# The exponentials' loads of the kernel generation: GpSimd's queue in place of SyncE's

## The chip, the cores and the metric

The kernel runs on one core of a Trainium2 chip. The core has five engines, each with its own instruction stream: TensorE (PE in the profile; its weight loads are PEld), VectorE (DVE), ScalarE (ACT), GpSimd (POOL) and SyncE (SP). SyncE, ScalarE and GpSimd also issue DMAs, which sixteen DMA engines carry out. The metric is the time of one execution on the device, in microseconds (us). TensorE's clock can be lowered by a throttle; the profile gives the granted clock as a share of full speed.

## The reference

The forward part, cut to what is computed; the kernel also returns the gradients for its twelve inputs, pulled back from `grad_out`.

```python
x = A_u                                            # 1 x 2048 x 576, bf16
xn = layernorm(x)
# state space branch
dt = exp(log_dt)[:, None]
P = exp((dt * A)[:, :, None] * arange(2048))       # A complex, 576 x 128
K = einsum("dn,dnl,dn->dl", C, P, dt * B).real     # one convolution kernel per channel
s = irfft(rfft(pad(xn)) * rfft(pad(K)))[:2048] + xn * Dskip
# gated branch
h = silu(xn @ w1) * (xn @ w3)                      # w1, w3: 576 x 4608
out = x + s * silu(h @ w2)                         # w2: 4608 x 576
...
out, vjp = jax.vjp(f, ...)
return out, *vjp(grad_out)
```

## The kernel before

The kernel is written with a framework that takes the program in the order in which Python produces it, gives each instruction a due time (`self.at(us)`), and lays out one fixed stream per engine from the due times and the data dependences. `issue_after` fixes an order between two instructions by hand, and `Chain` does so for a row of DMAs on one queue: each stands behind the one before it in the stream. Pools of buffers (`bufs=`) give the number of tiles of a name that may be in flight; a tile's load waits until the last reader of the tile that had its buffer is done.

The program has four parts: a preparation (layernorm, the spectrum of the input, and the exponentials of `early_exps`, which are stored to `E_dram`), then the stage with which this document deals, then the convolution with the second product of the gated branch, and the backward part.

In that stage two streams of work are interleaved.

*The kernel generation*, `ssm_kernel`, goes over 36 chunks of 16 channels with due times 6 us apart (TK). A chunk loads its exponentials E_l (L755; 128x1280 bf16, 320 KB, pool `kg_e` with three buffers) from `E_dram`. Then `kgen_chunk` makes five selector matmuls of the phases into PSUM (L776, et_ps, three buffers), ScalarE takes their sines into cs_k (L778, five instructions, two buffers), and VectorE multiplies and adds: p_k (L785), q_k (L789), two t_k (L797) and v_k (L801). In the streams, p_k and q_k are the first and the last reader of E_l. SyncE stores p_k for every second chunk (L787, `PZ_dram`) and q_k for each (L793, `Q_dram`, 512 KB). `kgen_sum` contracts q_k and v_k on TensorE (the kps products, L818) two chunks later, and copies the result to KT (L830). `phase_rows` (L726) fetches the phases' rows, lhs_t, in twelve small DMAs on SyncE, in front of the chunks 2, 11 and 20. At chunk 20 the matrix of the transform is made on VectorE and GpSimd (`dft_kernel_matrix`).

*The gate steps*, `ffn_hidden`, are 72, of two token tiles each, eight for every block of 512 hidden columns. A step multiplies with w1 and w3 (pg and pu, the matmuls of 128 rows in L1122, those of the last 64 rows, called tail matmuls here, in L1131). ScalarE makes s_t (silu, L1137) and u_t (L1142), VectorE g_t (L1141) and h_t (L1145). SyncE stores h_t (L1148), GpSimd stores g_t and u_t (L1151, 256 KB each). g_t, u_t, s_t and h_t have three buffers each. A block's weights are loaded once, on SyncE, into one of two buffers; those of the second block are chained behind `self.kg_load`, which at that point is the load of chunk 2. The gate steps start five ahead of the chunks, and `gate_mark` puts the first matmul of a step behind the last selector matmul of a chunk.

Some loads and stores for later stages also hang on `el`, the name that a chunk's E load has. `conv_loads`: at chunk 8 a row of Dskip and a store of a matrix, chained on SyncE; at chunk 12 the DMA copy `odd_grad_out`, within DRAM, on ScalarE's queue, behind the sine that was issued last (`self.sin_last`); at chunk 18 four transposes on SyncE. `turned_loads`: at chunk 25 a store, at chunk 30 eight transposes, all chained on SyncE.

SyncE's queue in this stage holds E loads, lhs_t loads, gate weights, PZ, Q and H stores and the chained ones, in one stream; each waits at the head of it for what it needs. GpSimd's holds the G and U stores.

Of the kernel before, what the change touches and what calls it, by code (L numbers as in the profile page):

```python
# [101 lines left out]
class K:  # L102
# [627 lines left out]
    def ssm_kernel(self, T0, TK, ps, ps1):  # L730
        nc, cfg = self.nc, self.cfg
        D, N = cfg.D, cfg.N
        NCH, H = D // 16, D // 2
        TW = 16 * (cfg.AV // 2 + cfg.BV)
        assert self.GE[-1] == NCH and cfg.AV == 2 * cfg.LT
        with self.pool(name="kg_l", bufs=2) as lp, \
                self.pool(name="kg_e", bufs=3) as ep, \
                self.pool(name="kg_qv", bufs=4) as qvp, \
                self.pool(name="kg_sb", bufs=2) as sb, self.pool(name="kg_dft", bufs=1) as dp:
            prev, lhs = [], [self.lhs_0]  # L740
            self.marks = []
            self.at(T0 - 3)
            self.write_weights(nc.scalar, self.WT[1], [self.W1[:, k] for k in range(2)])
            self.double_weights(nc.vector, self.WT[1])
            for ch in range(NCH):
                yield T0 + TK * ch
                self.at(T0 + TK * ch)
                if ch == 20:
                    self.dft_kernel_matrix(dp)
                if ch + 6 in self.GE[1:-1]:  # L750
                    lhs.append(self.phase_rows(len(lhs), lp, "lhs_t"))
                if ch in self.GE:
                    g = self.GE.index(ch)
                E = ep.tile([P, TW], BF16, name="E_l")
                el = self.kg_load = nc.sync.dma_start(out=E[:], in_=self.E_dram[ch // 4, :, ch % 4 * TW:(ch % 4 + 1) * TW])  # L755
                if ch in (8, 12, 18):
                    self.conv_loads(el, (8, 12, 18).index(ch))
                if ch in (25, 30):
                    self.turned_loads(el, (25, 30).index(ch))
                qv = self.kgen_chunk(ch, E, lhs[g][:, ch - self.GE[g], :], sb, qvp, ps)  # L760
                prev.append(qv)
                if ch >= 2:
                    self.kgen_sum(ch - 2, prev.pop(0), ps1, T0 + TK * ch, TK)
            for i in range(2):
                yield T0 + TK * (NCH + 0.5 * i)
                self.kgen_sum(NCH - 2 + i, prev.pop(0), ps1, T0 + TK * (NCH + 0.5 * i), TK * 0.5)

    def kgen_chunk(self, ch, E, lhs, sb, qvp, ps):
        nc, cfg = self.nc, self.cfg
        AV, BV = cfg.AV, cfg.BV  # L770
        DC, AP = 16, AV // 2
        QW, TW = DC * BV, DC * (BV + AP)
        CS = sb.tile([P, 2, TW], BF16, name="cs_k")
        for o in [QW, *range(0, QW, 256)]:
            pt = ps.tile([P, 2, 256], FP32, name="et_ps")
            ins = nc.tensor.matmul(pt[:], lhsT=lhs, rhs=self.SEL[:, :, o:o + 256], start=True, stop=True)  # L776
            with self.tc.issue_after(self.exps_last.ins):
                self.sin_last = nc.scalar.activation(out=CS[:, :, o:o + 256], in_=pt[:].bitcast(I16)[:, :, 0::2], func=ACT.Sin,  # L778
                                                     scale=6.283184 / 2 ** 16)
        self.marks.append(ins)  # L780
        q = qvp.tile([P, DC, 2, BV], BF16, name="q_k")
        if ch % 2 == 0:
            self.p2 = sb.tile([P, 2, 2, DC * AP], BF16, name="p_k")
        p = self.p2[:, ch % 2]
        nc.vector.tensor_tensor(out=p, in0=CS[:, :, QW:], in1=E[:, QW:][:, None].to_broadcast([P, 2, DC * AP]), op=ALU.mult)  # L785
        if ch % 2:
            nc.sync.dma_start(out=self.PZ_dram[:, ch - 1:ch + 1].rearrange("p j r x -> p (j r x)"),  # L787
                              in_=self.p2[:].rearrange("p j r x -> p (j r x)"))
        nc.vector.tensor_tensor(out=q[:].rearrange("p d k b -> p k d b"),  # L789
                                in0=CS[:, :, 0:QW].rearrange("p k (d b) -> p k d b", b=BV),  # L790
                                in1=E[:, 0:QW].rearrange("p (d b) -> p d b", b=BV)[:, None]
                                .to_broadcast([P, 2, DC, BV]), op=ALU.mult)
        nc.sync.dma_start(out=self.Q_dram[ch], in_=q[:].rearrange("p d k b -> p (d k b)"))  # L793
        t = sb.tile([P, 2, 2, DC, AV], BF16, name="t_k")
        for s in range(2):
            w = self.WT[s][:, ch].rearrange("p k r e u -> p (k r e) u")
            nc.vector.tensor_tensor(out=t[:].rearrange("p k r e (s a u) -> p (k r e) s a u", s=2, u=2)[:, :, s],  # L797
                                    in0=p.rearrange("p r (e a) -> p (r e) a", a=AP)[:, None].to_broadcast([P, 2, 32, AP]),
                                    in1=w[:, :, None, :].to_broadcast([P, 64, AP // 2, 2]), op=ALU.mult)
        v = qvp.tile([P, 2, DC, AV], BF16, name="v_k")  # L800
        self.v_last = nc.vector.tensor_tensor(out=v[:].rearrange("p k e a -> p k (e a)"),  # L801
                                              in0=t[:, :, 0].rearrange("p k e a -> p k (e a)"),
                                              in1=t[:, :, 1].rearrange("p k e a -> p k (e a)"), op=ALU.add)
        return q, v
# [1429 lines left out]
```

## Time and profile before

| what | value |
|---|---|
| time of the runs | 1758.15, 1758.81 and 1772.55 us, median 1758.81 |
| the profiled execution | 1755.24 us, of which the profile's span is 1753.1 |
| busy, share of the span | PE 1625.1 us (93%), DVE 1402.1 (80%), ACT 916.1 (52%), POOL 422.0 (24%) |
| hardware queue of SyncE's and ScalarE's DMAs | 565324 packets, 264.49 MB |
| software queue of GpSimd's DMAs | 37088 packets, 109.31 MB |

The stage in which both streams run goes from the first p_k, at 137.10 us, to the last, at 372.79. In front of it the gate steps run alone with the end of the preparation, behind it come the rest of the gate steps, the convolution and the backward part:

| stretch (us) | PE busy | DVE busy |
|---|---|---|
| 0 to 110 | 90.65 | 73.56 |
| 110 to 137 | 24.30 | 12.86 |
| 372.8 to 480 | 100.92 | 96.82 |
| 480 to 1753 | 1200.33 | 1014.99 |

How to read the rows that follow. A row of the timeline has start, duration, engine, line, operation, output and inputs, shapes, and the number of equal instructions that follow each other and are put in one row; in brackets stands the idle time in front of it and what ended it. SPq, ACTq and POOLq are the engines' DMA issues, where the duration is the issue and not the transfer. A row of the waits names the waiting instruction, what released it, the total, the number and the largest of these waits in the window. A row of the windows gives, for a stretch of time, the busy time of each engine with the number of its instructions, TensorE's mean granted clock, the DMA engines' busy share and the data rate.

### The profile page before, as it was taken

To read this page: it belongs to the slowest core of one execution; us is meant where nothing else is said; L and a number is where in the kernel's file an instruction comes from. 1 tells how busy PE (TensorE), PEld (TensorE's weight loads), DVE (VectorE), ACT (ScalarE), POOL (GpSimd) and SP (SyncE) were. 2 spreads that over 40 slices of the span, in tenths; PEclk is the share of its full clock that TensorE was granted. 3 is DMA by queue.
4 is the path that set the end of the run, shared out by engine and by line. 5 is a ranking of instruction groups with operands and counts; after the bars stand their busy time and mean duration, and the time that the engine had idled before them with its cause. 6 is when DMAs were issued, how large, how long until landed. Compare 5 with 4: busy or idle time off the path is not lost. (4 is left out here: it accounts for less than half of the span.)

```text
span 1753.1 us, 33144 instructions
## 1 busy us (share of the span) xinstructions
PE 1625.1 (93%) x12786; PEld 981.8 (56%) x12841; DVE 1402.1 (80%) x2170; ACT 916.1 (52%) x1674; POOL 422.0 (24%) x639
## 2 busy tenths in 40 slices
PE   7798788999997899889999999999999998999998
PEld 4453333444443677646555655555455566777766
DVE  6657798989894565587995899679799966899897
ACT  5667678777773111565866767565655501111111
POOL 7142121222223211111111212112121352122143
PEclk8899999999998999999999999999999999999999
DMA  6568897998778989848495776769899999999992
GB/s 204 208 210 288 287 314 257 322 340 259 254 264 208 232 208 191 225 144 235 146 278 161 206 205 202 196 172 268 196 262 225 251 222 240 227 205 216 231 201 51
DMA packets 624363, 394.86 MB, mean 225 GB/s; under 512 B 426798, under 2 KB 565678, under 8 KB 624206
## 3 DMA queue, kind: packets, MB, share of 16 engines
q1 hardware_dynamic: 565324, 264.49, 61.5%
q0 software_dynamic: 37088, 109.31, 19.8%
q10 hardware_dynamic: 21794, 18.95, 3.5%
q8 instruction: 100, 1.64, 0.4%
q14 instruction: 57, 0.47, 0.1%
HBM read 122.18 MB, written 182.13 MB: 174 GB/s over the span
## 5 line engine op out<-in xcount | busy, mean ns | idle before, releaser
L2017 PEld LDWEIGHTS <-acts 128*128 128x128 bf16 x2304 | 223.6, 98 | 63.9 <-issue 3.3
L1965 PE MATMUL pgw<-ggu,xn_bf 128*128 128x512 bf16 x1152 | 254.0, 379 | 0.1
L1122 PEld LDWEIGHTS <-xnT 128*128 128x128 bf16 x1152 | 107.8, 98 | 156.1 <-issue 53.5
L1500 DVE TENSOR_TENSOR pr_q<-et_ps,pz 128x1024 f32<-128x1024 f32 x144 | 176.0, 1223 | 21.1 <-PE et_ps L1494 11.9
L1965 PEld LDWEIGHTS <-xn_bf 128*128 128x128 bf16 x1152 | 111.5, 98 | 131.0 <-issue 0.4
L1504 DVE TENSOR_REDUCE S_b<-pr_q 128x64 f32<-128x1024 f32 x144 | 175.4, 1218 | 3.9
L1877 PE MATMUL ph<-w2T,goT 128*128 128x512 bf16 (+3 forms) x800 | 159.5, 368 | 10.6 <-DVE e L1237 3.7
L1122 PE MATMUL pg<-wmB_w,xnT 128*128 128x512 bf16 x539 | 151.5, 383 | 15.7 <-DVE g_t L1141 11.2
L1122 PE MATMUL pu<-wmB_w,xnT 128*128 128x512 bf16 x558 | 151.3, 383 | 1.7 <-issue 0.8
L1943 PE MATMUL pgw<-go_o,h_n 128*128 128x288 bf16 x1152 | 149.7, 287 | 1.1 <-ACT gh L1895 0.8
L1943 PEld LDWEIGHTS <-h_n 128*128 128x128 bf16 x1152 | 111.1, 98 | 31.2 <-issue 1.0
L1137 ACT ACTIVATE s_t<-pg 128x512 bf16<-128x512 f32 x144 | 87.2, 606 | 75.4 <-PE pu L1131 60.1
L2017 PE MATMUL px<-wT_ggu,acts 128*128 128x288 bf16 x896 | 123.5, 291 | 2.5 <-DMA wT_ggu<-in_B_w_dram 2.5
L1877 PEld LDWEIGHTS <-goT 128*128 128x128 bf16 (+1 forms) x800 | 65.0, 99 | 96.2 <-issue 41.1
L1151 POOL DMA_DIRECT2D G_dram<-g_t x72 | 52.3, 727 | 258.8 <-DVE g_t L1141 135.3
L1485 ACT COPY gz<-gz 64x1024 bf16<-64x1024 bf16 x36 | 37.6, 1043 | 147.1 <-DMA gz<-gK_dram 88.2
L2017 PE MATMUL px<-wA,acts 128*128 128x288 bf16 x832 | 109.8, 286 | 0.5 <-ACT gw13t L1980 0.5
L1971 POOL DMA_DIRECT2D out_dram<-gw x72 | 51.9, 722 | 207.6 <-ACT gw L1967 181.0
L778 ACT ACTIVATE cs_k<-et_ps 128x512 bf16<-128x512 int16 x180 | 93.2, 618 | 14.2 <-PE et_ps L776 11.5
L1948 POOL DMA_DIRECT2D out_dram<-gw x36 | 20.0, 555 | 330.6 <-ACT gw L1947 324.0
L1142 ACT CAST u_t<-pu 128x512 bf16<-128x512 f32 x144 | 86.4, 600 | 11.7 <-PE pu L1122 9.6
L1837 DVE TENSOR_TENSOR ggu<-ggu,h_n 128x1024 bf16<-128x1024 bf16 x72 | 48.9, 686 | 44.6 <-ACT ggu L1849 44.5
(341 smaller groups left out, 3190.4 us busy)
## 6 DMA issues: line engine op xcount, KB each, us to landing
G_dram<-g_t POOLq DMA_DIRECT2D x72, 256.0 KB, 4.5
U_dram<-u_t POOLq DMA_DIRECT2D x72, 256.0 KB, 4.7
H_dram<-h_t SPq DMA_DIRECT2D x72, 256.0 KB
Q_dram<-q_k SPq DMA_DIRECT2D x36, 512.0 KB
ggu<-G_dram POOLq DMA_DIRECT2D x18, 1024.0 KB, 8.1
h_n<-U_dram POOLq DMA_DIRECT2D x18, 1024.0 KB, 8.8
GG_dram<-ggu SPq DMA_DIRECT2D x36, 512.0 KB
GU_dram<-ggu SPq DMA_DIRECT2D x36, 512.0 KB
```

The lines of the kernel that those rows point to most:

```text
L778: self.sin_last = nc.scalar.activation(out=CS[:, :, o:o + 256], in_=pt[:].bitcast(I16)[:, :, 0::2], func=ACT.Sin, scale=6.283184 / 2 ** 16)
L1122: ins = nc.tensor.matmul(pt[:], lhsT=xnT[:, c, ts], rhs=wm[w][:, c, :], start=(q == 0 and c == 0), stop=(q == 1 and c == nfull - 1))
L1137: nc.scalar.activation(out=s_t[:, :, q, :], in_=pgv, func=ACT.Silu)
L1142: nc.scalar.copy(out=u_t[:, :, q, :], in_=puv)
L1151: self.u_stores[step] = nc.gpsimd.dma_start(out=dst[fb * ng:(fb + 1) * ng, i0 // 4, :, i0 % 4:i0 % 4 + NT, :].rearrange("g p t f -> p g (t ...
L1500: nc.vector.tensor_tensor(out=pr[:], in0=T[z][:].rearrange("p s k d f j -> p (s k) (d f j)")[:, None] .to_broadcast([P, 2, 4, 4 * AV]), in ...
L1504: nc.vector.tensor_reduce(out=self.sums_of[-1][:, :, :, z, :, dg, d0:d0 + 8].rearrange("p r s k d -> p (r s) k d"), in_=pr[:].rearrange("p ...
L1877: prev = nc.tensor.matmul(dst(j, k), lhsT=lw, rhs=rh, start=start, stop=stop)
L1943: self.pe_last = nc.tensor.matmul(pgw[pi_][:, 0:pw], lhsT=hn[:, tt, fl * P:(fl + 1) * P], rhs=self.go_o[:, tt, po:po + pw], start=(tt == 0 ...
L1965: self.pe_last = nc.tensor.matmul(pw_[:], lhsT=self.xn_bf[:, tt, c * P:(c + 1) * P], rhs=ggu[:, :, tt, :], start=(n == 0), stop=(n == LT - 1))
L1971: self.gp(lambda: nc.gpsimd.dma_start(out=aps[names[w]][(c - 1) * P:(c + 1) * P, fb:fb + FG].rearrange("(c p) f -> p c f", p=P), in_=gw[:, ...
L2017: self.pe_last = nc.tensor.matmul(px[pi_][:, 0:pw], lhsT=acts[i][:, ai, fi, :], rhs=w[:, po:po + pw], start=(n == 0), stop=(n == len(steps ...
```

## The change

Three edits. The E load goes from `nc.sync` to `nc.gpsimd`. The call of `kgen_chunk`, which stood after the hooks for later loads, stands before them. And `kg_load` and `el`, which named the E load of the chunk, now name its Q store, which is on SyncE: the second block's gate weights and the chained loads of `conv_loads` and `turned_loads` stand behind that instead. Since `kgen_chunk` has been called by then, `self.sin_last` in `conv_loads` is the last sine of chunk 12 instead of chunk 11. What is computed, the sizes and the buffers stay.

```diff
@@ -752,13 +752,14 @@
                 if ch in self.GE:
                     g = self.GE.index(ch)
                 E = ep.tile([P, TW], BF16, name="E_l")
-                el = self.kg_load = nc.sync.dma_start(out=E[:], in_=self.E_dram[ch // 4, :, ch % 4 * TW:(ch % 4 + 1) * TW])
+                nc.gpsimd.dma_start(out=E[:], in_=self.E_dram[ch // 4, :, ch % 4 * TW:(ch % 4 + 1) * TW])
+                qv = self.kgen_chunk(ch, E, lhs[g][:, ch - self.GE[g], :], sb, qvp, ps)
+                prev.append(qv)
+                el = self.kg_load = self.q_store
                 if ch in (8, 12, 18):
                     self.conv_loads(el, (8, 12, 18).index(ch))
                 if ch in (25, 30):
                     self.turned_loads(el, (25, 30).index(ch))
-                qv = self.kgen_chunk(ch, E, lhs[g][:, ch - self.GE[g], :], sb, qvp, ps)
-                prev.append(qv)
                 if ch >= 2:
                     self.kgen_sum(ch - 2, prev.pop(0), ps1, T0 + TK * ch, TK)
             for i in range(2):
@@ -790,7 +791,7 @@
                                 in0=CS[:, :, 0:QW].rearrange("p k (d b) -> p k d b", b=BV),
                                 in1=E[:, 0:QW].rearrange("p (d b) -> p d b", b=BV)[:, None]
                                 .to_broadcast([P, 2, DC, BV]), op=ALU.mult)
-        nc.sync.dma_start(out=self.Q_dram[ch], in_=q[:].rearrange("p d k b -> p (d k b)"))
+        self.q_store = nc.sync.dma_start(out=self.Q_dram[ch], in_=q[:].rearrange("p d k b -> p (d k b)"))
         t = sb.tile([P, 2, 2, DC, AV], BF16, name="t_k")
         for s in range(2):
             w = self.WT[s][:, ch].rearrange("p k r e u -> p (k r e) u")
```

## The prediction, made before the changed kernel ran

> **What bounds the kernel now.** I read the busy shares in three stretches first: the whole stage in which the change lies, and two stretches inside it where chunks follow each other evenly.
>
> ```profile
> core 0: us, PE busy (x) PEld busy (x) DVE busy (x) ACT busy (x) POOL busy (x), PEclk, DMA share, GB/s
> 137.10:372.80 235.70, 208.90 (x1923) 92.85 (x1955) 203.80 (x324) 180.44 (x357) 51.25 (x71) 0.97 0.89 301
> 230.80:268.00 37.20, 35.33 (x340) 16.20 (x345) 35.66 (x57) 30.75 (x62) 10.43 (x15) 1.00 0.96 318
> 329.70:372.80 43.10, 40.38 (x420) 18.89 (x428) 41.59 (x65) 33.85 (x68) 9.49 (x14) 1.00 0.99 312
> ```
>
> In the even stretches VectorE is busy 35.66 of 37.20 us (96%) and TensorE 35.33 (95%): the two together set the pace. Over the whole stage VectorE has only 203.80 of 235.70 us (86%). So time is lost somewhere between, and the starts of p_k, the first VectorE instruction of a chunk, show where (numbered 0 to 35 in order of time; here 8, 10, 13, 19, 20, 21, 22, 28 and 35):
>
> ```profile
> 188.43 0.41 DVE L785 TENSOR_TENSOR p_k<-cs_k,E_l 128x512 bf16<-128x512 bf16 x1
> 200.68 0.42 DVE L785 TENSOR_TENSOR p_k<-cs_k,E_l 128x512 bf16<-128x512 bf16 x1
> 230.89 0.42 DVE L785 TENSOR_TENSOR p_k<-cs_k,E_l 128x512 bf16<-128x512 bf16 x1
> 267.96 0.42 DVE L785 TENSOR_TENSOR p_k<-cs_k,E_l 128x512 bf16<-128x512 bf16 x1
> 289.84 0.41 DVE L785 TENSOR_TENSOR p_k<-cs_k,E_l 128x512 bf16<-128x512 bf16 x1
> 292.51 0.42 DVE L785 TENSOR_TENSOR p_k<-cs_k,E_l 128x512 bf16<-128x512 bf16 x1
> 295.79 0.42 DVE L785 TENSOR_TENSOR p_k<-cs_k,E_l 128x512 bf16<-128x512 bf16 x1
> 329.70 0.43 DVE L785 TENSOR_TENSOR p_k<-cs_k,E_l 128x512 bf16<-128x512 bf16 x1
> 372.79 0.42 DVE L785 TENSOR_TENSOR p_k<-cs_k,E_l 128x512 bf16<-128x512 bf16 x1
> ```
>
> The even pace is (267.96 - 230.89 + 372.79 - 329.70) / 13 = 6.17 us per chunk. From 10 to 13 it took 30.2 us instead of 18.5, and from 19 to 20 21.9 instead of 6.2. The waits and SyncE's queue around the first hole:
>
> ```profile
> 190.06 1.23 DVE L789 TENSOR_TENSOR q_k<-cs_k,E_l 128x2048 bf16<-128x2048 bf16 x1
> 208.15 2.63 SPq L726 DMA_DIRECT2D lhs_t<-PCS_dram  x5
> 208.29 0.79 ACTq L627 DMA_DIRECT2D odd_grad_out<-in_grad_out_dram  x1
> 210.82 10.98 SPq L755 DMA_DIRECT2D E_l<-E_dram  x3
> DVE p_k L785 <- DMA E_l<-E_dram: 10.3, 1, 10.3
> SPq L755 <- DMA odd_grad_out<-in_grad_out_dram: 8.8, 1, 8.8
> PE pg L1122 <- DVE g_t L1141: 11.2, 6, 9.2
> ```
>
> The buffer for chunk 11 was free when q_k of chunk 8 ended, at 190.06 + 1.23 = 191.29. But in SyncE's order that load stands behind the last of twelve small lhs_t loads, which are themselves strung between H and Q stores that wait for VectorE. It went out at 210.82. VectorE stood in front of p_k for 10.3 us, and TensorE, which needed g_t from behind that p_k, for 9.2. The second hole has the same queue in it: chunk 20's load is behind the next twelve.
>
> ```profile
> 277.50 0.34 SPq L755 DMA_DIRECT2D E_l<-E_dram  x1
> ```
>
> **The change part by part.** The instruction orders of the two programs say what moves. All 36 loads are on GpSimd's queue, one between the G and U stores of each gate step; GpSimd gets no other work, SyncE loses 36 issues, and the sizes stay. After the stage, the order on each engine is the old one. So the sum is made over the stage, and what it loses or gains passes to the end.
>
> *The holes.* Load c+3 now goes out when q_k of chunk c ends, past SyncE's lhs_t, H, Q and weight entries. What it has left until its p_k, from an even stretch (p_k and q_k of chunk 14, p_k of chunk 17):
>
> ```profile
> 236.75 0.42 DVE L785 TENSOR_TENSOR p_k<-cs_k,E_l 128x512 bf16<-128x512 bf16 x1
> 239.14 1.22 DVE L789 TENSOR_TENSOR q_k<-cs_k,E_l 128x2048 bf16<-128x2048 bf16 x1
> 255.43 0.42 DVE L785 TENSOR_TENSOR p_k<-cs_k,E_l 128x512 bf16<-128x512 bf16 x1
> L1151 POOL DMA_DIRECT2D U_dram<-u_t x41: 725/725/727, 111.3 to 384.2; - x41
> DMA to landing us min/median/max: 2.6/5.1/7.6
> L1200 POOL DMA_DIRECT2D w2g<-in_B_w_dram x6: 704/722/722, 547.9 to 552.2; - x6
> DMA to landing us min/median/max: 6.9/10.8/11.8
> ```
>
> 255.43 - 240.36 = 15.07 us, less 0.73 for the issue: 14.3 us. A GpSimd load of E does not exist in the trace. Stores of 256 KB on that queue in this very stage land in 2.6 to 7.6 us; loads of 288 KB, six issued in a row, in 6.9 to 11.8. I take 7.6, the same stage at the same load; both ends are below 14.3, so the load is hidden by three chunks of VectorE work. If that cover is gone, the excess is paid on VectorE.
>
> Here the Trainium skill speaks against the change: SBUF — State Buffer, section "SBUF: two separate sides", says that a DMA from GpSimd's queue is starved of descriptors while VectorE runs a two-port performance-mode instruction, and a later section gives about 620 against 3100 ns. The row above does not show it: 41 issues between 725 and 727 ns with VectorE 86% busy. By the rule, 2.5 us more would make 7.6 into 10.1, still an estimate under the slack, and the sum would be the same.
>
> Without late loads, chunks 8 to 35 take 27 x 6.17 = 166.6 us, plus VectorE's once-only work for the kernel matrix at chunk 20:
>
> ```profile
> 270.00:280.00 10.00, 2.61 (x3) 1.02 (x1) 1.00 0.72 235
> ```
>
> That is 2.6, and some 0.5 for five tiny ones beside it: 169.7 us against 372.79 - 188.43 = 184.4. **Gain 14.7 us.** The bounds are +-3.6, an even pace that is 0.13 off.
>
> *The uneven places left.* In the new order the kps products still split the selector matmuls near chunks 13 and 19. That costs between 0 (the piece 8 to 10 runs at 6.13 with such a split) and 2 us. I take 1.
>
> *A new late piece near the start.* kg_load now names a Q store. So the gate weights of the second block go out behind the Q store of chunk 2, where they went out behind its E load; and the order reacts: 18 selector matmuls (chunks 3 to 5 and part of 6) now stand ahead of step 8's first gate matmul, where eight stood. Step 8 before, and the price of a gate step without a chunk:
>
> ```profile
> 150.79 1.43 SPq L87 DMA_DIRECT2D wmB_w<-in_B_w_dram  x2
> 153.18 5.23 ACT L778 ACTIVATE cs_k<-et_ps 128x512 bf16<-128x512 int16 x10
> 156.02 1.02 PE L1122 MATMUL pg<-wmB_w,xnT 128*128 128x512 bf16 x4
> 158.23 1.02 PE L1122 MATMUL pu<-wmB_w,xnT 128*128 128x512 bf16 x4 [0.37 <-DMA wmB_w<-in_B_w_dram]
> 159.41 0.38 PE L1131 MATMUL pu<-wtail,xnT 64*128 64x512 bf16 x1
> 164.12 0.38 PE L1131 MATMUL pu<-wtail,xnT 64*128 64x512 bf16 x1
> 250.75 0.38 PE L1131 MATMUL pu<-wtail,xnT 64*128 64x512 bf16 x1
> ```
>
> ScalarE's ten cs_k from 153.18 end at 158.4; five more for chunk 5 make 161.0, which is when the gate group can start (156.02 before). Three cs_k of chunk 6 and the rest of the group give a last tail matmul at 164.2. Steps 9 to 11 have almost no selector work and cost 164.12 - 159.41 = 4.71 each: 178.3. Step 12 at the even 6.17: 184.5. p_k follows the last tail matmul by 255.43 - 250.75 = 4.7, so p_k of chunk 8 starts at 189.2 against 188.43. **Loss 0.8, taken as 1.** Ends: +5 if nothing of the late group is regained, and -6, since chunk 2's load no longer waits until 150 and one chunk could run a period earlier. The weights leave near 152 instead of 150.79; with the old 158.23 - 150.79 = 7.4 us they are there at 159.4, before step 8 wants them.
>
> *Waits on the queues.* On GpSimd a waiting load has the next G and U stores behind it, and these free g_t and u_t (three buffers each) for VectorE and ScalarE. In even running the load waits for q_k, which VectorE ends before that step's g_t, so nothing is added. Near the start loads 6 to 9 stand in a row ahead of step 8's stores, some 3 us late, under two spare buffers. On SyncE no entry waits longer. The grad_out copy follows chunk 12's sines instead of chunk 11's; the SyncE entry that waits for its completion lane is an H store instead of an E load.
>
> **Sum:** 14.7 - 1 - 1 = 12.7 us. The profiled execution took 1755.24 us (span 1753.1), which gives 1742.5; it is 3.6 under the median of 1758.81, so the forecast is 1746.1, 0.7% less. Its own range is 1742 to 1755: 16.6 to 4, with the ends above.
>
> **The rivals.** *The copy is paid elsewhere.* The odd_grad_out copy ran from 208.29 until SyncE got on at 221.8, much of it in the hole, while DMA engines are 0.96 to 0.99 busy in the even stretches. If it now costs some later transfer the same 10.3 us, 2.4 of 12.7 remain: 1756. Against it: 0.89 x 235.7 = 210 us of DMA work fits a stage of 223, and at a share of 0.99 chunks 28 to 35 still ran at the even pace. The skill's DMA: Bandwidth & Descriptors, section "Issuing engines are not separate DMA queues", has the three queues interleave on the same 16 engines and another queue save only issue time; by it nothing is gained beyond that, near this rival. I give it 16%.
>
> *The loads land late* (the other side). From 14.3 us of landing on, VectorE waits in every chunk: a buffer's round is issue 0.73, landing, and p_k to the end of q_k (240.36 - 236.75 = 3.6 for chunk 14), shared by three chunks. At 20 us the period is 24.3 / 3 = 8.1, or 1.9 x 27 = 52 more: 1798. At 16 us it is 6.8: 1762. For it: descriptors written by GpSimd, and a single queue shared with 72 stores. Against it: 11.8 is the slowest row. 14%, most of it above 1776.
>
> *VectorE never starves.* If the early piece runs evenly too, the stage is VectorE's 203.80 us at 96%, 212.6: 23 us less, 1736. The 18 selectors in a row speak against it. 9%.
>
> That the change does nothing is ruled out by the orders.
>
> **How the numbers follow.** Forecast 61%, the rivals 16, 14 and 9. The range 1738 to 1766 takes the forecast's own, the copy, and the near parts of the others; about 6% is left below and 12 above. One per cent is 17.6 us, about what a measurement can tell from no change: faster by that is the third rival and the forecast's edge, 0.11; slower is the late loads beyond 18 us of landing, 0.12; within it 0.77.
>
> **What would show it.** Right: no wait of p_k on E_l, p_k starts 6.2 apart from chunk 8 to 35 with one longer at 20, E loads landing in 5 to 10 us, the stage near 223 us, step 8's first gate matmul near 161. Wrong: p_k waiting for E_l in many chunks, issues on GpSimd far over 0.73 us, cs_k or g_t waiting for GpSimd's stores, step 8 waiting for weights, or gate steps elsewhere waiting for theirs behind Q stores; or a stage that is 12 us shorter with an end that isn't, the gain lost in the conv.

## The result, and the profile after

The changed kernel took 1741.31 us in the median of six runs (1735.57 to 1751.69); the kernel before took 1764.46 on the same chip (six runs, 1758.15 to 1772.55). The ratio is 0.9883, 95% interval 0.9846 to 0.9920. A second set, shown below, gave 0.9899 (0.9856 to 0.9943). The quotients of the medians are 0.9869 and 0.9873, inside these intervals. Three runs over 1.5% above the fastest of their kernel are not in the ratios of this document: 1792.93 us of the kernel before in the second set, 1774.98 with both groups of lhs_t loads moved, and 3255.66 with the weights behind the Q store of chunk 1, whose cause is not known. The profiled execution took 1742.17 us, of which the span is 1740.0. The forecast was 1746.1 and 0.7% less: inside the range, on the right side, and too small a gain.

The busy times of the changed kernel in the stretches that were shown of before, in the same columns: the stage from the first p_k to the last, chunks 13 to 19, and chunks 28 to 35.

```profile
132.89:356.99 224.10, 207.08 (x1932) 92.94 (x1965) 207.33 (x326) 181.67 (x361) 69.31 (x106) 0.99 0.94 319
217.65:256.04 38.39, 35.73 (x340) 16.17 (x345) 36.38 (x58) 31.13 (x64) 13.47 (x21) 1.00 0.96 346
313.90:356.99 43.09, 40.75 (x395) 18.64 (x401) 41.57 (x65) 35.66 (x72) 13.04 (x21) 1.00 0.96 324
```

The stage is 224.1 us long where it was 235.7, and VectorE is busy 93% of it instead of 86%. Its timeline shows p_k of chunks 8, 10, 13, 19, 20, 21, 25 and 35; behind them stands chunk 25 of the kernel before, which the prediction had not shown.

```profile
187.36 0.42 DVE L786 TENSOR_TENSOR p_k<-cs_k,E_l 128x512 bf16<-128x512 bf16 x1
199.56 0.42 DVE L786 TENSOR_TENSOR p_k<-cs_k,E_l 128x512 bf16<-128x512 bf16 x1
217.65 0.42 DVE L786 TENSOR_TENSOR p_k<-cs_k,E_l 128x512 bf16<-128x512 bf16 x1
256.04 0.42 DVE L786 TENSOR_TENSOR p_k<-cs_k,E_l 128x512 bf16<-128x512 bf16 x1
263.93 0.42 DVE L786 TENSOR_TENSOR p_k<-cs_k,E_l 128x512 bf16<-128x512 bf16 x1
271.43 0.42 DVE L786 TENSOR_TENSOR p_k<-cs_k,E_l 128x512 bf16<-128x512 bf16 x1
295.94 0.42 DVE L786 TENSOR_TENSOR p_k<-cs_k,E_l 128x512 bf16<-128x512 bf16 x1
356.99 0.42 DVE L786 TENSOR_TENSOR p_k<-cs_k,E_l 128x512 bf16<-128x512 bf16 x1
```

```profile
312.18 0.42 DVE L785 TENSOR_TENSOR p_k<-cs_k,E_l 128x512 bf16<-128x512 bf16 x1
```

From chunk 10 to 13 it is 18.1 us now instead of 30.2; the longest gaps left behind chunk 8 are at chunk 20 (7.9 and 7.5 us). The two programs, each profiled twice (the second profiles are the first two experiments), piece by piece in us:

| piece | before | before, again | after | after, again |
|---|---|---|---|---|
| start to p_k of chunk 8 | 188.4 | 190.8 | 187.4 | 187.0 |
| chunk 8 to 10 | 12.3 | 12.3 | 12.2 | 12.2 |
| chunk 10 to 13 | 30.2 | 30.2 | 18.1 | 18.1 |
| chunk 13 to 19 | 37.1 | 37.1 | 38.4 | 38.4 |
| chunk 19 to 25 | 44.2 | 44.2 | 39.9 | 39.9 |
| chunk 25 to 35 | 60.6 | 62.9 | 61.1 | 61.1 |
| last p_k to the end of the span | 1380.3 | 1390.6 | 1383.0 | 1378.4 |

So the stage ends 15.8 us earlier in the first pair (372.8 to 357.0) and 20.8 in the second (377.4 to 356.6). At the end of the stage the two profiles of before differ by 4.6 us and those of the changed kernel by 0.3; behind it they differ by 10.3 and 4.6.

The loads themselves, in the view of their tile: instructions with their durations in ns (least, median, most), what the issuing engine waited for, and the landing times.

```profile
L755 POOL DMA_DIRECT2D E_l<-E_dram x36: 537/554/601, 120.7 to 342.2; - x36
...
  DVE q_k L790: 90.6, 32
...
DMA to landing us min/median/max: 3.6/5.4/7.4
```

Thirty-two loads wait for q_k, as foreseen, and land in 3.6 to 7.4 us. Among VectorE's waits of the stage no p_k is left; the longest single one, the last figure of these rows, is 1.7 us.

```profile
DVE g_t L1142 <- ACT s_t L1138: 4.1, 7, 1.4
DVE h_t L1146 <- ACT u_t L1143: 2.6, 13, 0.5
DVE WTb L499 <- ACT WTb L493: 1.7, 1, 1.7
```

### The profile page after: what moved, and what is told of

It is laid out like the page before. It is cut to its first block, busy times and chain, and to the rows that moved or that the text cites. A ratio compares the mean times of both kernels' runs of the same rounds, so it can differ in the third digit from the quotient of the medians.

```text
span 1740.0 us, 33185 instructions
## 1 busy us (share of the span) xinstructions
PE 1621.5 (93%) x12784; PEld 981.9 (56%) x12841; DVE 1406.1 (81%) x2170; ACT 914.6 (53%) x1674; POOL 439.2 (25%) x675
```

## The experiments

Where no ratio is given, an experiment is one profiled execution.

**The two kernels again.** The first is the kernel before.

> The kernel before, unchanged, for a second profile of it. From the last p_k of the kernel generation to the end of the span took 1380.3 us before (372.79 to 1753.1) and 1383.0 after (356.99 to 1740.0), so 2.7 of the 15.8 us that the stage gained were given back behind it. Theory: that is scatter of single executions in the later stages, not a cost of the change. Then the stage repeats within 1 us (p_k of chunk 8 to p_k of chunk 35 about 184.4 us, p_k of chunk 11 waiting some 10 us for E_l), while the rest behind the stage comes out several us away from 1380.3. Rival, the change costs 2.7 us later: the rest repeats at 1380.3 within 0.5.

> The changed kernel, unchanged, for a second profile and a narrower ratio. Theory (scatter behind the stage): p_k of chunk 35 again at 357.0 within 1 us and the rest behind it several us away from 1383.0; the ratio then settles where the stage puts it, at 15.8 of 1760, so 0.991 (0.988 to 0.993). Rival (2.7 us are given back for good): the rest at 1383 within 0.5 and a ratio of 0.9925. If the ratio stays at 0.988, something else than the stage gains 5 us more.

The stage of the changed kernel repeats within 0.1 us from chunk 8 on; behind it the four profiles spread over 12 us, and neither kernel has a time of its own there. Nine further profiles below give 1377 to 1390 us for that part, whichever way the loads went. The 2.7 us are scatter. The ratio of this set, 0.9899 (median 1737.02 against 1759.29), is 17.8 us of 1759; both ratios agree with what the stage alone gives, 16 to 21. The second profile of before missed its expectation of 184.4: its stage from chunk 8 was 186.7 us, 2.3 longer in chunks 25 to 35. There an E load stands behind the eight gT transposes in SyncE's queue:

```profile
337.20 9.90 SPq L87 DMA_TRANSPOSE gT<-KS_dram  x6
347.20 0.52 SPq L793 DMA_DIRECT2D Q_dram<-q_k  x1
347.77 0.43 SPq L755 DMA_DIRECT2D E_l<-E_dram  x1
```

Six of them held the queue for 9.9 us, and VectorE waited 0.9 us for the E load behind them, then 1.6 us for cs_k at the next p_k, which was not followed up. The changed kernel has the transposes too, without an E load behind them.

**E on SyncE, the lhs_t loads on GpSimd.**

```diff
-                    lhs.append(self.phase_rows(len(lhs), lp, "lhs_t"))
+                    lhs.append(self.phase_rows(len(lhs), lp, "lhs_t", nc.gpsimd))
```

> The kernel before with the E loads left on SyncE; the twenty-four lhs_t loads of the groups in front of chunks 11 and 20, and those of chunk 2, go on GpSimd's queue instead. Theory, E loads were late because they stood behind the lhs_t loads in SyncE's order: no p_k waits for E_l, p_k of chunk 8 to p_k of chunk 35 takes 169.6 us within 2, as in the changed kernel, and since the order shows no group of eighteen selector matmuls ahead of step 8, chunk 8 starts 1 to 4 us before 187.4. Ratio 0.984 to 0.992. Rival, E loads are helped by GpSimd's queue itself (its own descriptors, another path): the piece stays near 184 us and the ratio is 0.997 to 1.003.

From chunk 8 to 35 it took 170.7 us (189.18 to 359.89), the ratio is 0.9906 (0.9871 to 0.9941). The loads' queue is not what gains; their place is. Against the expectation p_k waited for E_l twice, 1.6 us in all, for loads behind the gT transposes on SyncE. The start missed too (chunk 8 at 189.2): the first p_k came at 141.1, since the second block's weights now went ahead of the UH stores on SyncE, and WTb waited 4.7 us for one of those.

**Weights of the second block behind the Q store of chunk 1.**

```diff
-                el = self.kg_load = self.q_store
+                el, self.kg_load = self.q_store, self.q_store if ch < 2 else self.kg_load
```

> The changed kernel, but the second block's gate weights hang behind the Q store of chunk 1 instead of chunk 2. In the order the group of eighteen selector matmuls ahead of step 8 is gone; the rest of the stage's order is that of the changed kernel. Theory, this group costs some us that are regained only in part: step 8 ends near 157 instead of 162.7, chunk 8 starts at 183 to 186 instead of 187.4, and everything behind is as much earlier, 1 to 4 us under the changed kernel. Rival, the late step 8 is regained in full by chunk 8 (VectorE ran ahead with chunks 4 to 7), so the order costs nothing: chunk 8 at 187.4 within 0.5. Second rival, the weights arrive late (issue near 148 plus 7.4 of landing): TensorE waits for them at step 8 and chunk 8 is no earlier.

TensorE's waits around step 8:

```profile
PE pg L1123 <- DMA wmB_w<-in_B_w_dram: 4.1, 1, 4.1
PE pu L1123 <- DMA wmB_w<-in_B_w_dram: 1.0, 1, 1.0
```

The second rival it was: weights issued at 149.1 us, nothing to do for TensorE until they came, chunk 8 at 190.7 (3.4 later than in the changed kernel) and a ratio of 0.9941 (0.9911 to 0.9971). Some 4 us more were lost around chunks 16 to 18, where p_k waited 1.4 us for a PZ store; what made that store late was not followed up.

**Three quarters of the copy moved away.** The copy is cut in two; VectorE's order in the stage stays. The edit names chunk 30 for the second part, but nothing holds it there: in the program it was issued at 0.7 us, at the start. It is out of the stage either way.

```diff
-                nc.scalar.dma_start(out=self.odd["grad_out"][:], in_=self.turned(self.aps["grad_out"].flatten_outer_dims()))
+                nc.scalar.dma_start(out=self.odd["grad_out"][0:2], in_=self.turned(self.aps["grad_out"].flatten_outer_dims(), 0, 2))
...
+                if ch == 30:
+                    nc.scalar.dma_start(out=self.odd["grad_out"][2:], in_=self.turned(self.aps["grad_out"].flatten_outer_dims(), 2))
```

> The kernel before, but of the DRAM copy odd_grad_out only a quarter is made at chunk 12; the other three quarters follow at chunk 30. The order on VectorE through the stage is that of before. Theory, the first hole is chunk 11's place behind the lhs_t loads on SyncE: p_k of chunk 10 to p_k of chunk 13 stays at 27 to 30 us (30.2 and 30.2 in the two profiles of before), p_k of chunk 11 still waiting 8 us or more. Rival, the hole is the copy's traffic, and SyncE's wait of 8.8 us for it: the piece falls to 18.5 to 21 us.

Chunk 10 to 13 took 30.8 us (205.12 to 235.95), 0.8 over the upper end of the expectation, and the wait is longer than before:

```profile
DVE p_k L787 <- DMA E_l<-E_dram: 11.5, 1, 11.5
```

```profile
212.59 2.62 SPq L726 DMA_DIRECT2D lhs_t<-PCS_dram  x5
215.26 12.16 SPq L755 DMA_DIRECT2D E_l<-E_dram  x3
```

The load of chunk 11 is again the first entry behind the last five lhs_t loads. The copy's size does not make the hole. SyncE's wait for the copy stayed as well (10.2 us), but it lies behind that first E load.

**The other edits alone, E on SyncE.**

```diff
-                nc.gpsimd.dma_start(out=E[:], in_=self.E_dram[ch // 4, :, ch % 4 * TW:(ch % 4 + 1) * TW])
+                nc.sync.dma_start(out=E[:], in_=self.E_dram[ch // 4, :, ch % 4 * TW:(ch % 4 + 1) * TW])
```

> The changed kernel with one edit taken back: the E loads are on SyncE again, while the gate weights and the later loads still hang behind the Q stores. Theory, the gain is the E loads' way past SyncE's queue: in SyncE's order they stand behind the lhs_t loads again, so the two stretches in which chunks stand still come back (p_k of chunk 8 to p_k of chunk 35 at 180 to 190 us, 169.6 in the changed kernel) and the ratio is 0.995 to 1.005. Rival, hanging the weights and the other loads elsewhere is what gained: ratio 0.988 to 0.992, no such stretches.

Ratio 1.0031 (0.9997 to 1.0064). The stretch from chunk 8 to 35, here and, below it, in the changed kernel:

```profile
191.48:372.61 181.13, 164.87 (x1542) 72.69 (x1541) 159.78 (x255) 140.60 (x279) 40.72 (x57) 0.98 0.88 303
```

```profile
187.36:356.99 169.63, 158.14 (x1516) 72.00 (x1541) 161.32 (x254) 140.18 (x279) 53.70 (x82) 1.00 0.95 323
```

VectorE's busy time is 1.5 us less; it stood still for 21.4 us instead of 8.3, and the piece is 11.5 us longer. Both stretches are back (203.68 to 215.97 us at chunk 11, 266.84 to 289.75 at chunk 20), the first one smaller than before (24.7 us for chunks 10 to 13, not 30.2). No p_k waits for E_l behind chunk 8 here: the loads of chunks 11 and 20 stand behind the last lhs_t loads again (issued at 212.55 and 277.18 us), and the order has extra gate steps ahead of these chunks, so that VectorE waits for s_t and cs_k instead. The two edits bring nothing without the third.

**One group of lhs_t loads, then both, on GpSimd.** E stays on SyncE. The condition takes the group in front of chunk 20; in the second kernel it is `ch >= 5`, which takes that of chunk 11 too.

```diff
-                    lhs.append(self.phase_rows(len(lhs), lp, "lhs_t"))
+                    lhs.append(self.phase_rows(len(lhs), lp, "lhs_t", nc.gpsimd if ch == 20 else None))
```

> The kernel before with the E loads left on SyncE and one group of lhs_t loads, the twelve in front of chunk 20, on GpSimd's queue. The order differs from before only around chunk 20. It prices the second stretch alone: p_k of chunk 19 to p_k of chunk 25 took 44.2 us before and 39.9 in the changed kernel. Theory: 39 to 41 here, about 4 us gained, while chunk 10 to chunk 13 keeps its 30 us. The prediction had put this stretch at about 6 us (169.7 in all, of which 18.5 instead of 30.2 for the first). Rival, the stretch is due to the kernel matrix's work at chunk 20 alone, and stays at 43 or more.

> The kernel before with the E loads left on SyncE and both groups of lhs_t loads, in front of chunks 11 and 20, on GpSimd's queue; the first group, at chunk 2, stays on SyncE, and the early part of the order is that of before. Theory, all of the stage's gain behind chunk 8 is that E loads no longer stand behind lhs_t loads: p_k of chunk 8 to p_k of chunk 35 at 169.6 us within 2, chunk 8 itself at 188 to 191 as in the two profiles of before, the last p_k at 358 to 361 and a ratio of 0.988 to 0.993, the changed kernel's within the scatter. Rival, E loads on SyncE are late at other places too (behind H and Q stores that wait for VectorE): the piece stays over 173 us.

The first kernel's chunks 19 and 25:

```profile
268.76 0.42 DVE L785 TENSOR_TENSOR p_k<-cs_k,E_l 128x512 bf16<-128x512 bf16 x1
308.67 0.42 DVE L785 TENSOR_TENSOR p_k<-cs_k,E_l 128x512 bf16<-128x512 bf16 x1
```

That is 39.9 us, with 30.3 for chunks 10 to 13: the second stretch is worth 4.3 us and is the lhs_t loads' too. With both groups moved:

```profile
190.89:360.88 169.99, 160.91 (x1567) 71.90 (x1567) 161.22 (x255) 138.91 (x277) 47.31 (x68) 1.00 0.96 320
```

170.0 against 169.6 us in the changed kernel, with E still on SyncE, and a ratio of 0.9917 (0.9881 to 0.9953). Chunk 8 starts at 190.9, as in the kernel before, whose early order this is.

**Two buffers for E_l.**

```diff
-                self.pool(name="kg_e", bufs=3) as ep, \
+                self.pool(name="kg_e", bufs=2) as ep, \
```

> The changed kernel with two buffers for E_l instead of three. The prediction's slack of 14.3 us for a load becomes 14.3 - 6.2 = 8.1 us in the even stretches, and a load lands 3.6 to 7.4 us after its issue (median 5.4). Theory, the slack formula holds: p_k waits for E_l in no even stretch, p_k of chunk 8 to p_k of chunk 35 stays at 169.6 us within 2; only where chunks 4 to 7 follow each other at 3 to 4 us can a load be late, and that is regained by chunk 8. Rival, the three buffers are what hides GpSimd's loads: p_k waits in many chunks and the piece is over 175 us.

One wait in the whole stage, at chunk 5, and 169.7 us from chunk 8 to 35 (190.52 to 360.18):

```profile
DVE p_k L786 <- DMA E_l<-E_dram: 3.3, 1, 3.3
```

The prediction's slack of 14.3 us, less one period, holds in the even stretches. But the 3.3 us were not regained: g_t came late behind that p_k, TensorE waited 2.2 us for it, and chunk 8 started 3.2 us later than in the changed kernel.

**Weights behind the Q store of chunk 0.**

```diff
-                el = self.kg_load = self.q_store
+                el, self.kg_load = self.q_store, self.kg_load if ch else self.q_store
```

> The changed kernel, but the second block's gate weights hang behind the Q store of chunk 0 instead of chunk 2 (chunk 1 in weights_earlier, where they were issued at 149.1 and TensorE waited 4.1 and 1.0 us for them at step 8, with no selector matmuls left to fill that time). In this order they stand behind the Q store of chunk 1 at the latest and ahead of the lhs_t loads, so an issue near 141 to 146. Theory, with 7.4 us of landing they are there at 149 to 153, when step 8 wants them: no wait of TensorE for weights over 1.5 us, chunk 8 at 183 to 186 (187.4 and 187.0 in the changed kernel), the last p_k at 353 to 356 and a time 1 to 4 us under the changed kernel's. Rival, an earlier issue meets more traffic and the weights are no earlier, or another store behind them on SyncE is late: chunk 8 at 187 or later.

Now the weights were there (waits of 1.0 and 0.6 us), and the last tail matmul of step 8 came 4.0 us earlier than in the changed kernel. The last tail matmuls of steps 8, 9 and 12, here and then in the changed kernel (8 and 12):

```profile
158.73 0.37 PE L1132 MATMUL pu<-wtail,xnT 64*128 64x512 bf16 x1
164.61 0.38 PE L1132 MATMUL pu<-wtail,xnT 64*128 64x512 bf16 x1
183.13 0.38 PE L1132 MATMUL pu<-wtail,xnT 64*128 64x512 bf16 x1
```

```profile
162.74 0.38 PE L1132 MATMUL pu<-wtail,xnT 64*128 64x512 bf16 x1
183.28 0.38 PE L1132 MATMUL pu<-wtail,xnT 64*128 64x512 bf16 x1
```

By step 12 the 4.0 us are 0.15, and chunk 8 starts at 187.2. The rival's number came out, for a reason that neither side had named here: the eighteen selector matmuls are work that TensorE has to do anyway, ahead of step 8 or behind it. From 150 to 183.3 us the profiles show 25 selector matmuls in this kernel, in the changed one and in the kernel before; 21 of them come ahead of step 8's last tail matmul in the changed kernel, 5 here. The ratio, 0.9944 (0.9915 to 0.9973), is no better than the changed kernel's; 1.4 us were lost at chunks 13 to 19, where h_t waited 1.5 us for a store of H.

**E on ScalarE's queue.**

```diff
-                nc.gpsimd.dma_start(out=E[:], in_=self.E_dram[ch // 4, :, ch % 4 * TW:(ch % 4 + 1) * TW])
+                nc.scalar.dma_start(out=E[:], in_=self.E_dram[ch // 4, :, ch % 4 * TW:(ch % 4 + 1) * TW])
```

> The changed kernel with the E loads on ScalarE's queue instead of GpSimd's. In its stream a waiting load holds the sines and the copies behind it. Theory, the way past SyncE's lhs_t loads is what counts, and ScalarE, about 80% busy in the stage, can take the waits: p_k of chunk 8 to p_k of chunk 35 at 170 to 175 us, with no stretch of over 12 us between two p_k. Rival, each load waits for q_k in front of the next sines, VectorE and ScalarE then wait for each other, and the piece is 178 us or more.

It took 184.9 us from chunk 8 to 35, the rival's size by another way. From chunk 13 to 15 alone passed 26.4 us instead of the changed kernel's 13.6, which is 12.8 more, and ScalarE's timeline shows where:

```profile
216.06 5.09 ACTq L755 DMA_DIRECT2D E_l<-E_dram  x1
...
229.46 0.33 ACTq L755 DMA_DIRECT2D E_l<-E_dram  x1
229.83 0.60 ACT L1138 ACTIVATE s_t<-pg 128x512 bf16<-128x512 f32 x1 [7.56 <-DMA odd_grad_out<-in_grad_out_dram]
```

The copy odd_grad_out is on this queue; the issue behind it took 5.09 us instead of 0.33, and then ScalarE stood 7.6 us in front of s_t. Without those 12.8 us the piece would be near 172, against 169.6, so what the loads' waits cost by themselves looks small; but it was not run without the copy.

## Why the prediction was right, and where it was off

*The holes.* Forecast: 169.7 us for chunks 8 to 35 and 1 more for uneven places, 14.7 gained. Measured: 169.6 with the uneven places in, 14.7 in the first pair (184.4 - 169.6) and 17.0 in the second. The cause is shown from three sides: the holes stay, the first one smaller, when E stays on SyncE and only the chaining changes, they go when the lhs_t loads leave SyncE instead of the E loads, and the first doesn't go with most of the copy. The uneven place is there: chunks 13 to 19 take 1.3 us longer than before. The reading of the second hole was right in sum but not in kind: there VectorE waits for no load. The order had put two gate steps ahead of chunk 20, and part of its 21.9 us was regained by chunks 20 to 22; 4.3 is what it cost.

*The term that was off* is "a new late piece near the start", taken as a loss of 1 us. Chunk 8 came 1.1 us earlier in the first pair and 3.7 in the second. The sum put it at 189.2 us; it was at 187.4, 1.8 earlier. Of this, 1.5 us are step 8, whose last tail matmul was at 162.74 for 164.2. The sum let ScalarE's row of cs_k start at 153.18, where it stood in the kernel before, and it started 0.9 earlier:

```profile
152.31 10.58 ACT L779 ACTIVATE cs_k<-et_ps 128x512 bf16<-128x512 int16 x21
```

Another 0.6 is p_k, which followed the last tail matmul of step 12 by 4.1 us and not 4.7; steps 9 to 12 took 0.2 longer than in the sum. The late piece itself is there and costs nothing by step 12: the last tail matmul of step 8 came 3.3 us later than before (162.74 against 159.41), that of step 12 at 183.28 in both kernels. This is the row of the kernel before:

```profile
183.28 0.38 PE L1131 MATMUL pu<-wtail,xnT 64*128 64x512 bf16 x1
```

What the sum left out, and named only as an end of the range, is a hole in the old early part: chunk 2's load stands behind the first group of lhs_t loads.

```profile
145.70 0.35 SPq L726 DMA_DIRECT2D lhs_t<-PCS_dram  x1
...
148.75 1.61 SPq L726 DMA_DIRECT2D lhs_t<-PCS_dram  x3
150.41 0.34 SPq L755 DMA_DIRECT2D E_l<-E_dram  x1
```

Chunk 2's p_k started at 154.20, 11.7 us behind chunk 1's, and in the changed kernel at 146.87, 5.2 behind; with the three groups of lhs_t loads on GpSimd and E on SyncE it was 6.2 behind. As at chunk 20, hardly any wait for the load shows (0.2 us in the second profile, none in the first): the order has step 7's h_t ahead of that p_k. The hole shows in VectorE's busy time. These are 145 to 160 us and 165 to 187 us, in the kernel before and below it in the changed one:

```profile
145.00:160.00 15.00, 13.37 (x104) 5.43 (x106) 9.58 (x16) 12.02 (x25) 2.90 (x4) 1.00 0.91 308
165.00:187.00 22.00, 20.57 (x182) 9.15 (x182) 21.87 (x36) 17.73 (x36) 4.94 (x7) 1.00 1.03 364
```

```profile
145.00:160.00 15.00, 12.65 (x75) 4.34 (x74) 14.77 (x25) 13.50 (x29) 4.50 (x7) 0.89 1.02 349
165.00:187.00 22.00, 20.74 (x216) 9.97 (x219) 16.39 (x27) 13.32 (x27) 6.89 (x11) 1.00 0.95 330
```

Before, VectorE was busy 9.6 of the 15 us and then 21.9 of the 22: it was behind and set the time of chunk 8. In the changed kernel it had chunks 2 to 7 done early and could wait for the gate steps. This accounts for the 1.1 us of the first pair, though no run takes the early hole away by itself. In the second profile of before, TensorE also waited 1.7 us at step 8 for the second block's weights, which stand behind that same E load, and its last tail matmul there came 2.3 us later than in the first profile. Chunk 8 started at 188.4 to 192.9 us in five profiles with the old early order (the last is the run with the split copy, whose first p_k was already 4 us late), and at 187.4 and 187.0 in the changed kernel. The uneven places, 1 us in the sum, are inside the 169.6 and make the other part of the difference between 12.7 forecast and 15.8 measured in the first pair.

*The base.* The forecast took its gain from one profiled execution of before, 1755.24 us, which is shorter than all six runs behind the first ratio, and set it on a median of three runs, 1758.81, where six gave 1764.46. That the profiled execution of the changed kernel came out at 1742.17 for 1742.5 is luck in part: 3.1 us more were gained in the stage, 2.7 were lost to scatter behind it. The upper end of its own range, a gain of 16.6 us, is less than the ends that it names add up to (14.7 + 3.6 + 6 = 24.3); the lower end, 4, is their sum. The stage gained 15.8 and 20.8.

*The rivals.* The copy is not paid elsewhere: it ran from 212.58 us in the changed kernel, and VectorE was busy 9.31 of 10 us there.

```profile
209.00:219.00 10.00, 9.73 (x75) 4.41 (x75) 9.31 (x15) 7.89 (x16) 3.95 (x6) 1.00 0.95 300
219.00:229.00 10.00, 9.28 (x104) 4.22 (x104) 9.63 (x15) 7.09 (x15) 2.53 (x4) 1.00 1.00 385
```

The rule of the Trainium skill's DMA: Bandwidth & Descriptors, section "Issuing engines are not separate DMA queues", by which another queue saves only issue time, therefore did not set the time here: what was saved is neither bandwidth nor issue time but a place behind waiting entries. The loads did not land late: 5.4 us in the median and 7.4 at most, with 7.6 taken. The Trainium skill's SBUF — State Buffer, section "SBUF: two separate sides", would have GpSimd's DMAs starved of descriptors while VectorE runs a two-port performance-mode instruction; with VectorE busy 95% from chunk 8 to 35, the 36 issues took 537 to 601 ns, so no run here shows it. Whether VectorE's instructions in this stage are of that kind was not established. VectorE still starves a little (224.1 us of stage, not 212.6). "Faster by over 1%" had 0.11, and the two ratios lie at 1.2 and 1.0%: with the early hole in the sum it would have been nearer to an even chance.

## What to carry to other kernels

On a queue that is issued in order, a load that could go is held by every entry in front of it that still waits; so look, for each load that an engine waited for, when its buffer was free, when it was issued and what stood between, and move either of the two. Where an engine is the bound, reordering its own work cost nothing here as long as it did not stop (the eighteen selectors), while 3 us of waiting stayed in the time (the run with two buffers); so ask of a late piece whether the bounding engine stands still in it. When a change takes one hole away, look for all the places where the same queue order holds the same loads, the small ones too. They need not show as a wait for the load: where the order of the instructions already puts other work in front, they show as a late start and as waits for that work.

## What was not expected of the hardware

TensorE's granted clock fell after the standstill: here are the ten microseconds of the first hole in the kernel before and the ten behind it (the clock is the third figure from the end).

```profile
210.00:220.00 10.00, 2.91 (x29) 1.34 (x25) 1.99 (x3) 3.21 (x7) 0.72 (x1) 0.85 0.73 238
220.00:230.00 10.00, 7.69 (x55) 2.97 (x56) 8.48 (x15) 3.83 (x8) 0.72 (x1) 0.64 0.79 267
```

It was 0.85 and then 0.64 (0.81 and 0.68 in the second profile of before), and 1.00 at the same place of the changed kernel. The tail matmuls behind the hole took 0.60 to 0.63 us in the kernel before, where 0.38 is usual, so the hole can cost more than its length; how much it did was not measured. That it is the standstill which lowers the clock was not tested by itself, and a full stop is not needed: from 155 to 160 us the clock was 0.66 in the changed kernel, where TensorE was busy 4.66 of 5 us, all of it with the row of selector matmuls that follows ScalarE's sines (ScalarE busy 5.00).
